# Side steps of the first new pair in two lines, and block 3's operands staged in four tiles

## The chip, the cores and the metric

The kernel runs on one core of a Trainium2 chip. The metric is the device time of one execution in microseconds (us), a median over runs. The engines are TensorE (PE; PEld is its weight load), VectorE (DVE), ScalarE (ACT), GpSimd (POOL), and SyncE (SP), whose queue issues almost all DMAs here.

## What is computed

Three layers in a row, all in fp32 (the reference, cut):

```
qn, kn = q / norm over tokens, k / norm over tokens         # q, k, v: 6016 x 256
a = softmax(kn.T @ qn / tau);  x = v @ a                    # a: 256 x 256
h = relu(x @ w_in);            x = (h * h) @ w_out          # 256 -> 2048 -> 256
xn = x / rms(x) * rms_g
out = (silu(xn @ w_gate) * (xn @ w_val)) @ w_out2           # 256 -> 1536 -> 256
```

## The kernel before

Tokens are columns. They are cut into 12 blocks (ten of 512 tokens, two of 448), and two blocks make a pair (pairs 0 to 5). `v @ a @ w_in` is folded: the softmax gives a weight `m_h`, `m_l` at the start, so that the first MLP is one product with `m`, relu, square, and one with `w_out`. Every fp32 product is made of three matmuls on split operands (a high part `h` from a cast on ScalarE and a rest `l` from a subtraction on VectorE): high x high, high x low, low x high.

The order of every engine's instructions is that of the code: nothing is rescheduled, and each engine works off its own list in order. The stages:

- Attention statistics and weight preparation, then blocks 0 and 1 of the first MLP, and blocks 2 to 7 one by one (`mlp1`, 16 units each: six matmuls of the first product, then six of the second product of the unit three back). Beside the units run side steps given by tables (`hooks`, `beside`: unit number to functions): the RMS norm of the block before (`norm_steps`), the preparation of the next block's operands from v (`prep`), weight conversion (`conv_steps`), and `pair_steps`: the seven combinations of a normed pair that the second MLP's Strassen-like product needs. Each combination is split into a tile (`hi`: cast on ScalarE, then a DMA to DRAM, `xd`; `lo`: subtraction on VectorE, then a second DMA). The tile comes from `staged(...)`, which goes round a list of places; `ys` names two buffers, `p0`, `p1`, `p6` one each. A cast into a buffer must wait until both DMAs out of its previous content are done.
- Blocks 8 and 9 (pair 4, the first "new pair", `FIRST`) and 10 and 11 (pair 5) go through `mlp1_pair`: eight groups of seven products and eight second products (`down`). A group has three places, `aside()`, where side steps are taken from the list `side`: after the second product, after the fifth, and at the end. In pair 4 the side steps are the norm of block 7, the `pair_steps` of pair 3, and `v_steps`, which make pair 5's seven operand combinations from v and send them to DRAM (`vd`) by tiles of the same `first_stage` list (`ys`, `p6`, `ys`, ...). `fill` mixed both kinds into one list, in turn; in pair 4 two steps were taken at some places.
- The second MLP, pairs 0 to 5 (`mlp2`, 12 groups each), with side steps in pair 0: the norm and combinations of pair 5 (`pair_side`) and the conversion of the last rows of `w_out2` (`rows_steps`: `a` on GpSimd and ScalarE, `b0` to `b2` on VectorE, `h`, `l`). In the group in which the norm's small matmul takes a PSUM bank (`takes_bank`, then `root`), `rooted` stopped all further side steps.

PSUM has four banks `mm`: bank 0 is each group's first product, the other three turn by one from group to group, so the copy into `bu` (L1492 in `mlp2`) goes to the bank that the group before read last as `bv` (L1526).

Of the kernel before, what the change touches and what calls it, by code (L numbers as in the profile page):

```python
# [28 lines left out]
def attn_moe_kernel(ctx: ExitStack, tc, q, k, v, tau, w_in, w_out, w_gate, w_val, w2, rms_g, out):  # L29
# [9 lines left out]
    _, N, C = q.shape  # L39
# [6 lines left out]
    q, k, v = q[0], k[0], v[0]  # L46
# [9 lines left out]
    FIRST = NP - 2  # L56
# [989 lines left out]
    def pair_steps(p, stage, fine=False):  # L1046

        n = blocks[2 * p][1]
        st = {}

        def sub(o, a, b):
            def f():
                x = [xst[p][:, i, :n] for i in (o, a, b)]
                nc.vector.tensor_tensor(out=x[0], in0=x[1], in1=x[2], op=ALU.subtract)

            return f

        def hi(i):
            def f():
                st[i] = stage()[:, :, :n]  # L1060
                nc.scalar.copy(out=st[i][:, 0], in_=xst[p][:, i, :n])  # L1061
                if p not in x_dram:
                    x_dram[p] = dp.tile([P, NC7, 2, NB], F32, tag=f"x{p}", name="xd")
                nc.sync.dma_start(out=x_dram[p][:, i, 0, :n], in_=f32(st[i])[:, 0])

            return f

        def lo(i):
            def f():
                t = st.pop(i)  # L1070
                nc.vector.tensor_tensor(out=t[:, 1], in0=xst[p][:, i, :n], in1=f32(t)[:, 0], op=ALU.subtract)  # L1071
                nc.sync.dma_start(out=x_dram[p][:, i, 1, :n], in_=f32(t)[:, 1])

            return f

        def both(*fs):
            return lambda: [f() for f in fs] and None

        if fine:
            return [  # L1080
                only("act", hi(0)), only("dve", sub(3, 2, 0)), both(lo(0), hi(4)), only("dve", sub(1, 6, 3)),
                both(lo(4), hi(6)), only("dve", sub(2, 6, 2)), both(lo(6), hi(3)), only("dve", sub(5, 4, 1)),
                both(lo(3), hi(1)), both(lo(1), hi(2)), both(lo(2), hi(5)), only("dve", lo(5)),
            ]
        return [
            both(hi(0), sub(3, 2, 0)), both(lo(0), hi(4), sub(1, 6, 3)), both(lo(4), hi(6), sub(2, 6, 2)),
            both(lo(6), hi(3), sub(5, 4, 1)), both(lo(3), hi(1)), both(lo(1), hi(2)), both(lo(2), hi(5)),
            lo(5),
        ]
# [102 lines left out]
    def v_steps(p, into):  # L1192


        b, n = 2 * p, blocks[2 * p][1]
        st, raw = {}, {}

        def loads(t):
            def f():
                raw[t] = load_v(b + t)  # L1200

            return f

        def tr(t, kk):
            def f():
                if t == 0 and kk == 0:
                    x = vp.tile([P, KC, NB], F32, tag="vt", name="vt")[:, :, :n]
                    st["x"] = {0: x[:, 0], 4: x[:, 1], 5: x[:, 0]}
                if t == 1 and kk == 0:
                    a, c = (place(k, F32)[:, :, :n] for k in (0, 1))  # L1210
                    st["x"].update({2: a[:, 0], 6: a[:, 1], 3: c[:, 0], 1: c[:, 1]})
                x = st["x"][SLOT[t][kk]]
                nc.vector.transpose(out=x.rearrange("p (g t) -> p g t", t=32), in_=raw[t][:, :, kk, :])

            return f

        def sub(o, x, y):
            def f():
                nc.vector.tensor_tensor(out=st["x"][o], in0=st["x"][x], in1=st["x"][y], op=ALU.subtract)

            return f

        def hi(i):
            def f():
                st[i] = into(i, n)
                nc.scalar.copy(out=st[i][0], in_=st["x"][i])

            return f

        def lo(i):  # L1230
            def f():
                h, l, store = st.pop(i)
                nc.vector.tensor_tensor(out=l, in0=st["x"][i], in1=f32(h), op=ALU.subtract)
                if store:
                    store()

            return f

        def seq(*fs):
            return lambda: [f() for f in fs] and None  # L1240

        return [
            loads(0), tr(0, 0), seq(tr(0, 1), loads(1)), hi(0), seq(lo(0), hi(4)), lo(4),
            seq(tr(1, 0), sub(3, 2, 0)), seq(tr(1, 1), sub(1, 6, 3)), seq(hi(3), sub(2, 6, 2)),
            seq(lo(3), hi(1), sub(5, 4, 1)), seq(lo(1), hi(2)), seq(lo(2), hi(6)), seq(lo(6), hi(5)), lo(5),
        ]

    def first_place(ops):
# [42 lines left out]
    def mlp1_pair(p, ops, side, after_product, after_group):  # L1291
# [43 lines left out]
        def group(g):  # L1335
# [5 lines left out]
                after_product(g, i)  # L1341

            def aside(k=1):
                for _ in range(k):
                    if side and not getattr(side[0], "takes_bank", False):
                        x = side.pop(0)()
                        if x:
                            x()

# [12 lines left out]
                old[2]()  # L1362
            down_slot()
            product(3, S1, bh, True)
            aside(2 if p == FIRST and g < G // 2 else 1)
            down_slot()
            product(1, S2, bu, False)
            uw = work(F32)[:, :, :n]
# [33 lines left out]
                r, q = x[:, 0], x[:, 1]  # L1402
            sums(TENSOR_ADD_SAT, out=r, in0=bh, in1=u, s0=FMAX, s1=0.0)
            lo()
            aside(2 if p == FIRST or g % 2 else 1)
            down_slot()
            left.append(square(r, q, f0, 1, False, last, 4))
            after_group(g)
# [7 lines left out]
    def mlp2(p, ops, after_product, after_group, side):  # L1416
# [17 lines left out]
        def group(f):  # L1434
# [26 lines left out]
            rooted = []  # L1461

            def aside(*only):
                if not side or rooted or getattr(side[0], "takes_bank", False):
                    return None
                e = getattr(side[0], "only", "")
                if not only or e in only:
                    side.pop(0)()
                    return e
# [205 lines left out]
    for b in range(2, 2 * FIRST):  # L1675
# [15 lines left out]
            else:  # L1691
                hooks = merge(hooks, {7: n0, 8: n1[:1], 9: n1[1:2], 10: n1[2:3], 13: n1[3:4], 14: n1[4:5], 15: n1[5:]})
        if b > 2 and b % 2:
            x = pair_steps(b // 2 - 1, staged("ys") if b == 3 else staged("ys", "p0", "ys", "p1"))
            beside = merge(beside, at_steps(x, {3: 4, 2 * FIRST - 1: 0}.get(b, 1)))
        if b < 2 * FIRST - 1:
            x = prep(b + 1)
            hooks = merge(hooks, {0: [load(b + 1)]} if b > 2 else {})
            at = (8, 9, 10, 11) if b % 2 else (3, 4, 8, 9)
            beside = merge(beside, {u: [f] for u, f in zip(at, x)})  # L1700
        else:
            beside.setdefault(0, []).append(third)
            x = v_steps(FIRST, first_place(ops1))
            for u in (0, 1, 3, 5, 6, 7, 8, 9, 10, 11, 12, 13, 14, 15):
                beside.setdefault(u, []).append(x.pop(0))
        for u in range(UNITS):
            if b in CONV:
# [11 lines left out]

    ops0 = {}  # L1720
    n0, n1 = norm_steps(2 * FIRST - 1, ys[2 * FIRST - 1])
    side = []

    def alternate(x, y):
        return [f for i in range(max(len(x), len(y))) for f in x[i : i + 1] + y[i : i + 1]]

    def fill():
        n = n0 + n1
        rest = side[:]
        k = len(n)  # L1730
        side[:] = alternate(n, rest[:k]) + pair_steps(FIRST - 1, first_stage) + rest[k:]

    drained.append(fill)
    first_stage = staged(*["ys", "p6", "ys"] * 4, "ys", "ys")
    for p in range(FIRST, NP):
        nxt = {}
        last = p == NP - 1
        if not last:
            side += v_steps(p + 1, through_dram(p + 1, first_stage))

        def after_product(g, i):
            if g == NF1 // 2 - 1:
                if not last and i in ORDER[3:]:
                    fetch_v(p + 1, i, nxt)
                if last and i == 0:
                    fetch(0, 4, ops0)

        def after_group(g):
            if g == 0 and p > FIRST:
                side.extend(pair_norm(p - 1) + pair_steps(p - 1, staged("ys", "p0", "ys", "p1")))  # L1750
            if not last and g == NF1 // 2 - 2:
                assert len(side) <= 4, len(side)
                for i in ORDER[:3]:
                    fetch_v(p + 1, i, nxt)
            if last:
                if g == 0:
                    nc.sync.dma_start(out=f32(gv_chunk(1)), in_=gv_dram[1])
                if g == NF1 // 2 - 2:
                    assert not side, len(side)
                    for i in ORDER[:3]:  # L1760
                        fetch(0, i, ops0)
                if g == NF1 // 2 - 1:
                    for i in (2, 5, 6):
                        fetch(0, i, ops0)

        mlp1_pair(p, ops1, side, after_product, after_group)
        ops1 = nxt
# [23 lines left out]
        ]  # L1791
    pair_side = pair_norm(NP - 1) + pair_steps(NP - 1, staged("vt", "ys", "vraw", "ys"), True)
    side = []
    side += pair_side[:6] + alternate(rows_steps, pair_side[6:])

    def load_w2(f, k):
        for j, x in enumerate("hl"):
# [5 lines left out]
    for p in range(NP):  # L1803
# [6 lines left out]
        def after_group(f):  # L1810
            if p == 0:
                if f == 0:
                    for x in "hl":
                        tiles[f"w2_{x}"] = wp.tile([P, NF2, KC, 4, 32], F32R, tag=f"w2_{x}", name=f"w2_{x}")
                    load_w2(0, 2 * EARLY)
                    late_calls[0].load()
                    for i in (2, 3, 4, 5):
                        nc.sync.dma_start(out=f32(gv_chunk(i)), in_=gv_dram[i])
            if f == 10 and p == 0:
# [61 lines left out]
```

## Time and profile before

| | us |
|---|---|
| median of 3 runs (lowest, highest) | 1134.37 (1133.78, 1135.11) |
| the profiled execution's own time | 1134.62 |
| span of its instructions | 1132.8 |
| PE busy / PEld busy | 1113.6 / 933.7 |
| DVE busy / ACT busy / POOL busy | 779.0 / 788.3 / 73.1 |

Busy time is what an engine spends in instructions; a matmul of the trace overlaps the next one (a row with 0.39 us stands 0.23 us before the next), so the start of a row tells more of the pace than its length. A row in brackets, `[3.67 <-DMA xd<-xp]`, says that the engine stood idle so long before the instruction and what ended it. Times are from the span's start.

### The profile page before, as it was taken

How to read it: one execution, taken by the hardware profiler on the slowest of the kernel's cores; microseconds unless marked ns; L12 is line 12 of the kernel's file. 1: busy time of each engine (PE TensorE's matmuls, PEld its weight loads, DVE VectorE, ACT ScalarE, POOL GpSimd, SP SyncE). 2: the span in 40 equal slices, each digit the busy share in tenths (PEclk: the TensorE clock that was granted, in tenths of full speed). 3: DMA queues.
4: the chain of work that ended last, by engine and by line, in shares of the span. 5: the costliest groups of instructions: out<-in, count | busy, mean ns of one | idle time of the engine just before them, and what ended most of it. 6: DMA issues, size and time to landing. Idle time of an engine off the chain costs nothing.

```text
span 1132.8 us, 14576 instructions
## 1 busy us (share of the span) xinstructions
PE 1113.6 (98%) x5170; PEld 933.7 (82%) x5170; DVE 779.0 (69%) x1194; ACT 788.3 (70%) x1428; POOL 73.1 (6%) x106
## 2 busy tenths in 40 slices
PE   8999999999999999999999999999999999999997
PEld 7978888877888888768997888888888888888996
DVE  6998768878878787766866875555555655655655
ACT  7688778778888787667778766556556566556554
POOL 2421102102111000000000000000000000000000
PEclk9999999999999999989999999999999999999999
DMA  9643321353343331135168242202302302202001
GB/s 327 221 112 95 111 71 60 112 180 99 132 148 102 122 100 49 63 143 185 45 207 343 62 150 79 84 1 75 93 1 75 93 1 75 68 19 66 19 19 34
DMA packets 103305, 114.47 MB, mean 101 GB/s; under 512 B 50368, under 2 KB 71872, under 8 KB 102592
## 3 DMA queue, kind: packets, MB, share of 16 engines
q1 hardware_dynamic: 100960, 112.68, 29.9%
q10 hardware_dynamic: 2272, 0.85, 0.3%
q8 instruction: 41, 0.67, 0.3%
q14 instruction: 32, 0.26, 0.1%
HBM read 71.83 MB, written 41.68 MB: 100 GB/s over the span
## 4 chain that ended last, share of the span: by engine, by line
PE 55%; DVE 1%; ACT 0%; DMA 0%; issue 0%; DVEq 0%; ACTq 0%
PE mm L1441 30%; PE acc L110 7%; PE acc L111 7%; PE acc L112 7%; PE mm L1339 4%; DMA vd<-xp 0%; PE acc L1569 0%; DVE xp L1071 0%; DMA xd<-xp 0%; DVE p L1326 0%; DVE sh L1329 0%; ACT xp L1061 0%; DVE p L1071 0%; ACT mm L1370 0%; DVE p L1382 0%
## 5 line engine op out<-in xcount | busy, mean ns | idle before, releaser
L1441 PE MATMUL mm<-p,gv 128*128 128x512 f32 (+1 forms) x1188 | 302.3, 387 | 0.0
L1441 PEld LDWEIGHTS mm<-p,gv 128*128 128x128 f32 x1188 | 221.7, 188 | 45.7 <-DVE hp L1517 1.1
L1542 DVE TENSOR_TENSOR sh<-hp,sh 128x512 fp32r<-128x512 f32 (+1 forms) x144 | 98.0, 681 | 138.2 <-ACT sh L1538 137.9
L1492 ACT COPY mm<-mm 128x512 f32<-128x512 f32 (+1 forms) x72 | 40.4, 562 | 172.2 <-PE mm L1441 163.0
L111 PE MATMUL acc<-sh,wo_h 128*128 128x512 f32 (+1 forms) x384 | 149.6, 390 | 2.9 <-DVE sh L849 2.2
L110 PE MATMUL acc<-sh,wo_h 128*128 128x512 f32 (+1 forms) x384 | 149.9, 390 | 1.1 <-ACT sh L1320 1.1
L112 PE MATMUL acc<-sh,wo_l 128*128 128x512 f32 (+1 forms) x384 | 148.9, 388 | 0.1
L849 DVE TENSOR_TENSOR sh<-p,sh 128x512 fp32r<-128x512 f32 x128 | 92.7, 726 | 55.3 <-ACT sh L842 48.9
L110 PE MATMUL acc<-sh,w_h 128*128 128x512 f32 (+1 forms) x284 | 109.5, 386 | 0.0
L112 PE MATMUL acc<-sh,w_l 128*128 128x512 f32 (+1 forms) x284 | 109.5, 385 | 0.0
L111 PE MATMUL acc<-sh,w_h 128*128 128x512 f32 (+1 forms) x284 | 109.5, 385 | 0.0
L837 ACT ACTIVATE p<-mm 128x512 f32<-128x512 f32 x128 | 76.0, 594 | 25.2 <-PE mm L112 24.9
L1538 ACT CAST sh<-hp 128x512 fp32r<-128x512 f32 (+1 forms) x144 | 89.1, 618 | 3.4 <-DVE hp L1526 1.9
L112 PE MATMUL mm<-p,m_l 128*128 128x512 f32 x224 | 87.5, 391 | 0.3 <-DVE m_l L773 0.3
L111 PEld LDWEIGHTS acc<-sh,wo_h 128*128 128x128 f32 x384 | 72.6, 189 | 18.5 <-DVE sh L849 4.4
L110 PE MATMUL mm<-p,m_h 128*128 128x512 f32 x224 | 87.3, 390 | 0.0
L111 PE MATMUL mm<-p,m_h 128*128 128x512 f32 x224 | 87.2, 389 | 0.0
L110 PEld LDWEIGHTS acc<-sh,wo_h 128*128 128x128 f32 x384 | 72.6, 189 | 15.0 <-ACT sh L1320 1.5
L112 PEld LDWEIGHTS acc<-sh,wo_l 128*128 128x128 f32 x384 | 72.5, 189 | 14.3 <-DVE wo_l L182 0.9
L1441 PE MATMUL mm<-xs,gv 128*128 128x512 f32 (+1 forms) x324 | 82.6, 381 | 0.0
L1526 DVE TENSOR_TENSOR hp<-mm,sg 128x512 f32<-128x512 f32 (+1 forms) x72 | 48.9, 679 | 44.3 <-PE mm L1441 44.3
L1517 DVE TENSOR_TENSOR hp<-mm,pu 128x512 f32<-128x512 f32 (+1 forms) x72 | 49.0, 681 | 30.0 <-ACT pu L1516 30.0
(249 smaller groups left out, 2080.3 us busy)
## 6 DMA issues: line engine op xcount, KB each, us to landing
p<-xd SPq DMA_DIRECT2D x58, 256.0 KB, 4.0
xd<-xp SPq DMA_DIRECT2D x46, 256.0 KB, 2.0
gv<-gvd SPq DMA_DIRECT2D x5, 1792.0 KB, 16.3
gvd<-gp SPq DMA_DIRECT2D x15, 512.0 KB, 3.3
xd<-p SPq DMA_DIRECT2D x24, 256.0 KB, 2.2
raw<-in_moe_w_out_dram SPq DMA_DIRECT2D x11, 512.0 KB, 3.7
out_dram<-ot SPq DMA_DIRECT2D x40, 128.0 KB, 2.3
qraw<-in_q_dram SPq DMA_DIRECT2D x13, 384.0 KB, 7.2
```

The source lines that it names most:

```text
L110: nc.tensor.matmul(o, wh, xh, start=start, stop=False)
L111: nc.tensor.matmul(o, wh, xl, start=False, stop=False)
L112: nc.tensor.matmul(o, wl, xh, start=False, stop=stop)
L837: nc.scalar.activation(out=r, in_=o, func=AF.Relu)
L849: nc.vector.tensor_tensor(out=sl, in0=s, in1=f32(sh), op=ALU.subtract)
L1339: nc.tensor.matmul(bank, m_part(a, w, g), x, start=start and j == 0, stop=j == 2, skip_group_check=not start)
L1441: nc.tensor.matmul(bank, c[:, hl, a, fs], x, start=start and j == 0, stop=j == 2, skip_group_check=not start)
L1492: cp(out=bu, in_=b0)
L1517: add(out=h22, in0=bh, in1=w, op=ALU.add)
L1526: dve(out=h21, in0=bv, in1=sg1, op=ALU.mult)
L1538: nc.scalar.copy(out=parts[t][0], in_=x)
L1542: dve(out=pl, in0=x, in1=f32(ph), op=ALU.subtract)
```

## The change

- Pair 4's side steps stand in two lists, `side` (norm and `pair_steps`) and `tokens` (`v_steps`); a place takes one of each, but only one step that casts into a staging tile (`staged`): the second waits for the next place. In pair 5 the same rule holds for the two steps of a place.
- `v_steps` has 15 steps (its `lo(1)` and `hi(2)` are apart); block 7, which runs the same steps by a table, takes two of them at unit 11.
- Block 3's `pair_steps` go round `ys, p0, ys, p1` (four buffers) in place of `ys` alone (two). `p0` and `p1` hold block 4's operands later, so their splits in `prep` move from units 10 and 11 to 12 and 13.
- In pair 0 of `mlp2`, VectorE-only steps may follow the root in the same group; the first late row is converted earlier, and its load stands ahead of `load_w2`.

```
@@ mlp1_pair
             def aside(k=1):
-                for _ in range(k):
-                    if side and not getattr(side[0], "takes_bank", False):
-                        x = side.pop(0)()
+                staged = False
+                for q in [side] * k + [tokens]:
+                    if q and not getattr(q[0], "takes_bank", False):
+                        if staged and getattr(q[0], "staged", False):
+                            break
+                        f = q.pop(0)
+                        staged = getattr(f, "staged", False)
+                        x = f()
                         if x:
                             x()
...
             product(3, S1, bh, True)
-            aside(2 if p == FIRST and g < G // 2 else 1)
+            aside()
...
             lo()
-            aside(2 if p == FIRST or g % 2 else 1)
+            aside(1 + (p > FIRST and g % 2))
@@ v_steps
-            seq(lo(3), hi(1), sub(5, 4, 1)), seq(lo(1), hi(2)), seq(lo(2), hi(6)), seq(lo(6), hi(5)), lo(5),
+            seq(lo(3), hi(1), sub(5, 4, 1)), lo(1), hi(2), seq(lo(2), hi(6)), seq(lo(6), hi(5)), lo(5),
@@ mlp2
             def aside(*only):
-                if not side or rooted or getattr(side[0], "takes_bank", False):
+                if not side or getattr(side[0], "takes_bank", False):
                     return None
                 e = getattr(side[0], "only", "")
+                if rooted and e != "dve":
+                    return None
@@ blocks 2 to 7
         if b > 2 and b % 2:
-            x = pair_steps(b // 2 - 1, staged("ys") if b == 3 else staged("ys", "p0", "ys", "p1"))
+            x = pair_steps(b // 2 - 1, staged("ys", "p0", "ys", "p1"))
...
-            at = (8, 9, 10, 11) if b % 2 else (3, 4, 8, 9)
+            at = (8, 9, 12, 13) if b == 3 else (8, 9, 10, 11) if b % 2 else (3, 4, 8, 9)
...
-            for u in (0, 1, 3, 5, 6, 7, 8, 9, 10, 11, 12, 13, 14, 15):
+            for u in (0, 1, 3, 5, 6, 7, 8, 9, 10, 11, 11, 12, 13, 14, 15):
@@ pairs 4 and 5
-    def fill():
-        n = n0 + n1
-        rest = side[:]
-        k = len(n)
-        side[:] = alternate(n, rest[:k]) + pair_steps(FIRST - 1, first_stage) + rest[k:]
-
-    drained.append(fill)
+    side, tokens = [], []
+    drained.append(lambda: side.extend(n0 + n1 + pair_steps(FIRST - 1, first_stage)))
...
-            side += v_steps(p + 1, through_dram(p + 1, first_stage))
+            tokens += v_steps(p + 1, through_dram(p + 1, first_stage))
@@ side steps of pair 0 in mlp2
-    side += pair_side[:6] + alternate(rows_steps, pair_side[6:])
+    x, y = rows_steps[1:], pair_side[6:]
+    side += pair_side[:5] + rows_steps[:1] + pair_side[5:6] + [f for i in range(max(len(x), len(y))) for f in x[i : i + 1] + y[i : i + 1]]
...
+                    late_calls[0].load()
                     load_w2(0, 2 * EARLY)
-                    late_calls[0].load()
```

TensorE's list is the same in both kernels. Three places where the other lists differ (line numbers of the changed kernel are a few higher).

**ScalarE in block 3, units 9 to 11.** L837 begins a unit's evacuation, L1061 is the cast of `hi`, L106 the cast of block 4's operand. Before:

```order
L1061 CAST xp<-xst 128x512
L837 ACTIVATE p_828<-mm 128x512
L841 ACTIVATE p_829<-p_828 128x512
L842 CAST sh<-p_829 128x512
L1061 CAST xp<-xst 128x512
L106 CAST p_2328<-vt 128x512
L837 ACTIVATE p_828<-mm 128x512
L841 ACTIVATE p_829<-p_828 128x512
L842 CAST sh<-p_829 128x512
L106 CAST p_2329<-vt 128x512
L145 ACTIVATE raw<-raw 128x512
```

and now:

```order
L1061 CAST p_2301<-xst 128x512
L837 ACTIVATE p_828<-mm 128x512
L841 ACTIVATE p_829<-p_828 128x512
L842 CAST sh<-p_829 128x512
L1061 CAST xp<-xst 128x512
L837 ACTIVATE p_828<-mm 128x512
L841 ACTIVATE p_829<-p_828 128x512
L842 CAST sh<-p_829 128x512
L145 ACTIVATE raw<-raw 128x512
L837 ACTIVATE p_828<-mm 128x512
L845 ACTIVATE sh<-p_828 128x512
L106 CAST p_2373<-vt 128x512
```

Every second cast of `hi` goes to a tile `p`, and the two casts L106 stand two units later.

**ScalarE in pair 4, the end of one group and the start of the next.** L1393 (now L1410) reads the sixth product, L1358 (now L1375) is the next group's first copy, L1226 a cast of `v_steps`, L1061 one of `pair_steps`. Before, from the end of group 3 on:

```order
L1393 ACTIVATE p_4014<-mm 128x512
L1320 ACTIVATE sh<-p_4014 128x512
L1324 ACTIVATE p_4015<-p_4014 128x512
L1226 CAST xp<-p_4252 128x448
L1061 CAST p_4362<-xst 128x512
L1358 COPY mm<-mm 128x512
L1320 ACTIVATE sh<-p_4014 128x512
L1061 CAST xp<-xst 128x512
L1370 COPY mm<-mm 128x512
L1371 COPY sh<-mm 128x512
```

and now the same stretch:

```order
L1410 ACTIVATE p_4014<-mm 128x512
L1332 ACTIVATE sh<-p_4014 128x512
L1336 ACTIVATE p_4015<-p_4014 128x512
L1061 CAST xp<-xst 128x512
L1375 COPY mm<-mm 128x512
L1332 ACTIVATE sh<-p_4014 128x512
L1061 CAST xp<-xst 128x512
L1387 COPY mm<-mm 128x512
L1388 COPY sh<-mm 128x512
```

Each place now casts into one staging tile where this one cast into two.

**VectorE in pair 4, group 2, and in pair 0 of `mlp2`, group 2.** L929 is the reciprocal of the norm, L1213 (now L1219) a transpose of v, L1329 (now L1341) the rest `l` of the square that the next group's first `down` reads. Before:

```order
L1382 ISA p_4013<-mm,sh 128x512
L929 RECIPROCAL ns<-ns 128x16
L1213 STREAM_TRANSPOSE p_4251<-vraw 128x448
L1219 TENSOR_TENSOR p_4252<-p_4251,vt 128x448
L1329 TENSOR_TENSOR sh<-p_4015,sh 128x512
```

and now, with the norm's transpose L938 between:

```order
L1399 ISA p_4013<-mm,sh 128x512
L929 RECIPROCAL ns<-ns 128x16
L938 STREAM_TRANSPOSE p_4095<-p_4095 128x512
L1219 STREAM_TRANSPOSE p_4214<-vraw 128x448
L1225 TENSOR_TENSOR p_4215<-p_4214,p_4215 128x448
L1341 TENSOR_TENSOR sh<-p_4015,sh 128x512
```

In `mlp2`, L998 is the reciprocal of the root and L1526 (now L1545) the product that reads the bank `bv`. Now:

```order
L1536 TENSOR_TENSOR hp<-mm,pu 128x512
L998 RECIPROCAL ns<-ns 128x28
L149 TENSOR_SCALAR sg<-sg 128x512
L153 ISA sg<-pu,sg 128x1024
L1545 TENSOR_TENSOR hp<-mm,sg 128x512
```

L149 and L153 (the late row's first conversion) stood two groups further on.

## Rows read from the trace of the kernel before

**Rows 1.** The page, part 1: busy time of each engine (share of the span).

```profile
PE 1113.6 (98%) x5170; PEld 933.7 (82%) x5170; DVE 779.0 (69%) x1194; ACT 788.3 (70%) x1428; POOL 73.1 (6%) x106
```

**Rows 2.** Waits of TensorE over the span: us in total, times, longest.

```profile
PE mm L1339 <- ACT mm L1358: 2.2, 1, 2.2
PE acc L111 <- DVE sh L849: 2.2, 4, 1.1
```

**Rows 3.** Busy time in three stretches of pair 4: stretch, length, engines, PEclk, DMA.

```profile
455.50:465.70 10.20, 10.20 (x46) 8.45 (x45) 9.46 (x16) 7.51 (x15) 0.00 (x0) 1.00 0.00 0
475.90:480.00 4.10, 2.27 (x8) 1.28 (x8) 1.29 (x2) 3.29 (x7) 0.00 (x0) 0.98 0.22 84
480.00:490.60 10.60, 8.38 (x21) 5.99 (x20) 4.40 (x7) 4.29 (x9) 0.00 (x0) 0.53 0.38 148
```

**Rows 4.** TensorE in order of time: first matmuls of groups 5, 6, 7 and of pair 5.

```profile
475.96 0.39 PE L1339 MATMUL mm<-vx,m_h 128*128 128x512 f32 x1
...
494.76 0.39 PE L1339 MATMUL mm<-vx,m_h 128*128 128x512 f32 x1
...
505.90 0.39 PE L1339 MATMUL mm<-vx,m_h 128*128 128x512 f32 x1
...
516.10 0.36 PE L1339 MATMUL mm<-p,m_h 128*128 128x448 f32 x1
```

**Rows 5.** SP and ScalarE in order of time, pair 4, group 5.

```profile
474.62 0.32 SPq L1072 DMA_DIRECT2D xd<-xp  x1
...
476.68 0.62 ACT L1061 CAST xp<-xst 128x512 fp32r<-128x512 f32 x1 [3.67 <-DMA xd<-xp]
```

**Rows 6.** Busy time in block 3's late units and block 4's first.

```profile
240.00:261.00 21.00, 18.84 (x78) 13.90 (x77) 17.41 (x25) 17.91 (x32) 4.93 (x6) 1.00 0.45 140
```

**Rows 7.** Waits of ScalarE from 218 to 262 us.

```profile
ACT xp L1061 <- DMA xd<-xp: 6.7, 4, 2.7
```

**Rows 8.** TensorE in order of time: the same matmul of a unit, six units apart.

```profile
240.66 0.39 PE L110 MATMUL mm<-p,m_h 128*128 128x512 f32 x1
...
261.07 0.39 PE L110 MATMUL mm<-p,m_h 128*128 128x512 f32 x1
```

**Rows 9.** Pair 0 of mlp2 in order of time: ScalarE, VectorE and TensorE.

```profile
606.94 0.57 ACT L1492 COPY mm<-mm 128x512 f32<-128x512 f32 x1 [1.81 <-DVE hp L1526]
...
615.28 0.58 ACT L1492 COPY mm<-mm 128x512 f32<-128x512 f32 x1
...
614.14 0.63 DVE L1526 TENSOR_TENSOR hp<-mm,sg 128x512 f32<-128x512 f32 x1
...
621.71 0.42 DVE L149 TENSOR_SCALAR sg<-sg 128x512 int32<-128x512 int32 x1
622.25 0.69 DVE L153 CUSTOM_DVE_ANT_0 sg<-pu,sg 128x1024 uint16<-128x1024 uint16 x1
...
616.09 1.55 PE L1441 MATMUL mm<-p,gv 128*128 128x512 f32 x6
```

**Rows 10.** The late row's load: SP, landing of all three, and TensorE's first matmul with w_l.

```profile
593.27 0.48 SPq L134 DMA_DIRECT2D pu<-in_moe_w_out_dram  x1
...
DMA to landing us min/median/max: 3.5/4.1/9.0
...
603.59 0.39 PE L112 MATMUL acc<-sh,w_l 128*128 128x512 f32 x1
```

**Rows 11.** VectorE and TensorE in order of time: block 7's norm, and pair 4's group 2.

```profile
420.89 0.24 DVE L929 RECIPROCAL ns<-ns 128x16 f32<-128x16 f32 x1
...
422.46 0.65 DVE L844 TENSOR_TENSOR p<-p 128x512 f32<-128x512 f32 x1
...
453.99 0.68 DVE L1329 TENSOR_TENSOR sh<-p,sh 128x512 fp32r<-128x512 f32 x1
...
456.42 0.39 PE L111 MATMUL acc<-sh,wo_h 128*128 128x512 f32 x1
```

More of the change, by code (lines that the diff above doesn't have):

```diff
@@ L1064, in f @@
                 nc.sync.dma_start(out=x_dram[p][:, i, 0, :n], in_=f32(st[i])[:, 0])
+            f.staged = True
             return f
@@ L1076, in both, with g @@
         def both(*fs):
-            return lambda: [f() for f in fs] and None
+            def g():
+                for f in fs:
+                    f()
+            g.staged = any(getattr(f, "staged", False) for f in fs)
+            return g
         if fine:
@@ L1226, in f @@
                 nc.scalar.copy(out=st[i][0], in_=st["x"][i])
+            f.staged = True
             return f
@@ L1239, in seq, with g @@
         def seq(*fs):
-            return lambda: [f() for f in fs] and None
+            def g():
+                for f in fs:
+                    f()
+            g.staged = any(getattr(f, "staged", False) for f in fs)
+            return g
         return [
@@ L1721, in attn_moe_kernel @@
     n0, n1 = norm_steps(2 * FIRST - 1, ys[2 * FIRST - 1])
-    side = []
-    def alternate(x, y):
-        return [f for i in range(max(len(x), len(y))) for f in x[i : i + 1] + y[i : i + 1]]
-    def fill():
-        n = n0 + n1
-        rest = side[:]
-        k = len(n)
-        side[:] = alternate(n, rest[:k]) + pair_steps(FIRST - 1, first_stage) + rest[k:]
-    drained.append(fill)
+    side, tokens = [], []
+    drained.append(lambda: side.extend(n0 + n1 + pair_steps(FIRST - 1, first_stage)))
     first_stage = staged(*["ys", "p6", "ys"] * 4, "ys", "ys")
@@ L1751, in after_group @@
             if not last and g == NF1 // 2 - 2:
-                assert len(side) <= 4, len(side)
+                assert not side and len(tokens) <= 3, (len(side), len(tokens))
                 for i in ORDER[:3]:
```

## The prediction

> **What bounds the kernel now.** The page comes first: TensorE is busy 1113.6 of 1132.8 us, the next engine 788.3 [rows 1]. So the end moves only by what TensorE stands still or runs slowly, and a step on another engine costs nothing as long as TensorE does not wait for it. Next I asked where it waits. Apart from the start (the first 80 us, which the change does not touch) the list of waits holds two places: pair 4 in `mlp1_pair`, where a matmul waited 2.2 us for ScalarE's copy L1358, and the end of block 3, where four second products waited 2.2 us in sum for VectorE's L849 [rows 2].
>
> Pair 4: the stretches show group 3 running at 10.20 us with TensorE never idle; then 1.83 us of 4.10 are idle in one stretch and 2.22 of 10.60 in the next, and there the granted clock is 0.53, that is mostly the lower level of 1.2 GHz; elsewhere it is 1.00 [rows 3]. The reader is to see both in the starts of the groups: group 7 takes 505.90 to 516.10 = 10.20 us, which is the pace, but groups 5 and 6 together take 475.96 to 505.90 = 29.94 us, **9.54 us too long** [rows 4].
>
> What holds ScalarE there? A cast into a `ys` tile. VectorE's `lo` of the tile's previous content is done and its store is issued at 474.62; the cast starts when it has landed, at 476.68, after 3.67 us of standing still [rows 5]. Behind that cast in ScalarE's list are the square that the next second product reads, then the copy that the next product needs: TensorE waits, VectorE waits for ScalarE, the next `lo` and its store come later, and the next cast later still.
>
> Block 3 has the same cause earlier: four casts waited 6.7 us for stores [rows 7], because `ys` alone gives a tile back after two units. ScalarE falls behind, and when the conversion of weights fills it and VectorE some units later (17.91 and 17.41 of 21 us) TensorE runs dry [rows 6]. Its idle time there is 21.00 - 18.84 = 2.16 us [rows 6]. But I size the loss from starts: the same matmul of a unit stands at 240.66 and, six units later, at 261.07, that is 20.41 us [rows 8]. A unit is 12 matmuls, and a group has 45 in 10.20 us [rows 4], so six units take 16.32: **4.09 us too long**.
>
> The Trainium skill (Perfetto Trace Analysis, Identifying the Most-Contended Engine) says that matmul busy share is a poor measure of headroom and weight-load busy share a good one. It holds here: weight loads are 8.45 of 10.20 us at full pace and 13.90 of 21.00 in this stretch [rows 3, 6], which would make 4.2 us lost, near the 4.09; by idle time alone the sum below would be 1123.7 in place of 1121.8.
>
> **The change, part by part.** TensorE's list stays as it is, so every gain is a wait taken away.
>
> 1. *One staging tile at a place, two lists.* The three tiles of `first_stage` go round, and a group has three places, so a tile is asked for again one group later, about 10 us. Cast, `lo` at the next place (about 3.4 us on), store (474.62 to 476.68, 2.06 us [rows 5]): some 6 us, 4 to spare. The tightest is a `ys` tile whose `lo` stands at the middle place and which the next group's first place wants: seven of a group's fifteen slots of 0.68 us lie between, 4.8 us, and ScalarE has a copy and a square before it (1.1 us), against two steps of VectorE ahead of the store (1.2 us), 0.5 us of issue and the store's 2.1 us or a little more: 1 to 2 us to spare. I take all of it: -9.54, waits, the low clock and the restarts. Bounds: -9.54 if no cast waits; about -3.5 if a shorter wait returns and the clock falls again (rival 1).
>
> 2. *VectorE is fuller in groups 2 and 3.* It was busy 9.46 of 10.20 us in group 3 [rows 3] already. In group 2 the norm's transpose now stands ahead of the v transpose and of `lo` L1329. The pair reciprocal and transpose with ScalarE's copy between took 420.89 to 422.46 = 1.57 us [rows 11]. So `lo`, at 453.99, starts at most at 455.56 and ends at 456.24. The matmul that reads it starts at 456.42 [rows 11], its weight load some 0.2 us before: it just fits, or is late by a little. In group 3, seven side steps of VectorE (16 instructions in 9.46 us [rows 3] make 0.59 each) put the same `lo` as close. Bounds: 0 to 0.3 us at each of the two; I take +0.2 in sum.
>
> 3. *Block 3 in four tiles.* A tile comes back after four units (10.9 us) in place of two (5.4), so the 6.7 us of waits go. The two splits of block 4 move to units 12 and 13, into the fuller stretch, and add two casts (0.5 us each) and two subtractions (0.6 each) there, where ScalarE would now be early by most of 6.7 us. They must end before block 4's first matmul, three units on. Of the 4.09 us some 0.15 stay, the norm's two small matmuls. I take -3.94. Bounds: -2 (half of the lateness is VectorE's conversion, not the tiles) to -4.09.
>
> 4. *Pair 0 of `mlp2`.* L149 and L153 now stand behind the reciprocal and ahead of L1526 in the root's group. Their busy times are 0.42 + 0.69 us [rows 9], so L1526 moves from 614.14 to 615.25 and ends at 615.94. The next group's copy into `bu` waits for it (in the group before it waited 1.81 us for just this [rows 9]): it starts at 615.94, not 615.28, and with 0.57 us ends at 616.51. TensorE wants that bank at 616.09 [rows 9]: +0.45 (0.42 and a restart). Bounds: 0, if the end of the copy counts less than its busy time, to 0.7. What is queued behind the copy on ScalarE shifts by as much and hides in its idle time. The late row's load, now first: before, it was issued at 593.27 as the last of the three and took 9.0 us, so all three are in by 602.3 in either order, and the first matmul that wants `w_l` is at 603.59 [rows 10]: nothing, unless the queue gives up 1.3 us.
>
> 5. *Block 7 (two steps at unit 11) and pair 5 (deferred casts)*: TensorE does not wait there before, and VectorE gets 0.6 us one unit earlier: nothing, covered by the three-unit lag of the second products.
>
> Sum, against the profiled execution's 1134.62 us: -9.54 + 0.2 - 3.94 + 0.45 = -12.83, so 1121.8. The median of the runs is 0.25 lower, so **1121.5**.
>
> **Rivals.**
>
> 1. *New short waits bring the low clock back once.* For it: in pair 4 the clock fell right after TensorE had stood 1.83 us in one short stretch [rows 3], and part 2 leaves next to no margin at two group ends. Against it: in block 3 it stood 2.16 us in 21 and kept 1.00 [rows 6]. Price: of the 9.54 us, 1.83 + 2.22 = 4.05 were idle in the two stretches [rows 3]; the other 5.5 are the clock, the restarts and a last short wait. I take 5.0 for the clock and restarts, and 1.0 of new waits: 1127.5. The Trainium skill (TensorE: Matmul & The Clock Gate, A second HAM failure mode: psum-queue depth-cycling) describes this: frequent micro-idles between groups make the clock swing. By that rule waits as short as part 2's could be enough; block 3's stretch speaks against it.
>
> 2. *Block 3 stays late.* The conversion on VectorE, not the tiles, holds it, and the moved splits add to it. For it: VectorE is busy 17.41 of 21 us [rows 6]. Price: 2 us of the gain: 1123.5.
>
> 3. *One of the two places does not do what it says*: the casts wait for something else than their tile. Against it: the waits name the stores [rows 5, 7]. Price: pair 4 alone missing, 1131; block 3 alone missing, 1125.5. Both missing is no change.
>
> 4. *Slower.* One mechanism: the short waits of part 2 come at each of pair 4's eight group ends, since VectorE never catches up. A spell at the low clock costs the same 5.0 + 1.0 us; slower than before needs more than 12.8 us above the forecast, so from the third spell on, 1140 or so. Against it: outside groups 2 and 3 the lists have at most five side steps in a group, with the group's own eight or nine 14 instructions of 0.59 us, 8.3 of 10.2 us, so VectorE catches up in group 4.
>
> **How the numbers follow.** No change here means within 0.2% (2.3 us), about what a measurement of this kernel can tell. The forecast (1120.6 to 1123.2): 0.67. Rival 1: 0.13. Rival 2: 0.09. Rival 3: 0.05 with one place missing, 0.03 with both (no change). Rival 4: 0.03. Faster is all but the last two, 0.94. The forecast and rival 2 hold 0.76, so the range reaches to rival 1: 1120.4 to 1127.8, which leaves out some 0.11. The low end is every cost at nothing, the rest of the small matmuls included.
>
> **What would show it.** In the changed profile: the granted clock at 1.00 through pair 4 and its groups at 10.2 us each; no cast L1061 or L1226 waiting for a store there or in block 3; block 3's six units near 16.4 us; no wait of TensorE for L849; one wait of some 0.4 us for ScalarE's copy in `mlp2`, pair 0, group 3; perhaps one or two below 0.3 us for a `lo` at the start of pair 4's groups 3 and 4. I am wrong if a stretch at 0.5 shows up in pair 4, if a cast still waits over 1 us for a store, or if VectorE's transposes of pair 4 push a second product by more than 0.5 us.

## The result, and the profile after

The changed kernel takes 1121.96 us (median of 4 runs, 1120.95 to 1122.38) against 1134.08 (4 runs, 1133.78 to 1135.11): ratio 0.989, 95% interval 0.9873 to 0.9907. The forecast was 1121.5, in a range of 1120.4 to 1127.8. The profiled execution took 1122.16 us, its span is 1120.5.

The page, part 1 (answers to [rows 1]), and all waits of TensorE that the profile names after the first 85 us (answers to [rows 2]; us in total, times, longest):

```profile
PE 1107.9 (99%) x5170; PEld 931.7 (83%) x5170; DVE 779.8 (70%) x1194; ACT 789.6 (70%) x1428; POOL 74.5 (7%) x106
```

```profile
PE mm L1458 <- ACT mm L1511: 0.3, 1, 0.3
```

Both waits of before are gone, and one that was not there has come, in `mlp2`.

**Pair 4.** The stretches of groups 3, 4, 5 and 6 (as [rows 3]) and the first matmuls of groups 5, 6, 7 and of pair 5 (as [rows 4]):

```profile
451.49:461.69 10.20, 10.20 (x47) 8.45 (x45) 9.86 (x17) 8.17 (x16) 0.00 (x0) 1.00 0.19 72
461.69:471.89 10.20, 10.20 (x47) 8.45 (x45) 9.73 (x16) 8.25 (x16) 0.00 (x0) 1.00 0.50 191
471.89:482.09 10.20, 10.20 (x47) 8.45 (x45) 7.76 (x13) 8.33 (x16) 0.00 (x0) 1.00 0.39 151
482.09:492.29 10.20, 10.20 (x47) 8.45 (x45) 6.93 (x12) 7.79 (x15) 0.00 (x0) 1.00 0.32 125
```

```profile
471.89 0.39 PE L1351 MATMUL mm<-vx,m_h 128*128 128x512 f32 x1
...
482.09 0.39 PE L1351 MATMUL mm<-vx,m_h 128*128 128x512 f32 x1
...
492.29 0.39 PE L1351 MATMUL mm<-vx,m_h 128*128 128x512 f32 x1
...
502.49 0.36 PE L1351 MATMUL mm<-p,m_h 128*128 128x448 f32 x1
```

Groups 3 to 7 take 10.20 us each, with no idle time and the clock at 1.00: groups 5 and 6 take 20.40 us where they took 29.94. And no cast waits for a store any more (where [rows 5] had 3.67 us); these are all waits of ScalarE from 415 to 505 us, and the ones for TensorE mean that ScalarE is early:

```profile
ACT mm L1387 <- PE mm L1351: 9.6, 7, 2.1
ACT p L1391 <- PE mm L1351: 3.0, 8, 1.0
ACT mm L1375 <- PE mm L1351: 2.8, 4, 0.9
ACT sh L1332 <- DVE p L1399: 2.8, 6, 0.8
ACT p L937 <- DVE ns L929: 1.6, 2, 0.8
```

**Block 3.** The same matmuls as in [rows 8], six units apart, and ScalarE's waits from 216 to 262 us (as [rows 7]):

```profile
240.49 0.39 PE L110 MATMUL mm<-p,m_h 128*128 128x512 f32 x1
...
257.06 0.39 PE L110 MATMUL mm<-p,m_h 128*128 128x512 f32 x1
```

```profile
ACT gp L211 <- DVE dg L157: 2.7, 1, 2.7
ACT p L837 <- PE mm L112: 2.0, 6, 0.5
ACT p L937 <- DVE ns L929: 0.8, 1, 0.8
```

16.57 us in place of 20.41, and no line `<- DMA` is left. L837 now waits for TensorE: the order of who waits for whom has turned.

**`mlp2`, pair 0, group 2 and the start of group 3** (as [rows 9]): VectorE, ScalarE, TensorE in order of time.

```profile
601.37 0.36 DVE L149 TENSOR_SCALAR sg<-sg 128x512 int32<-128x512 int32 x1
601.77 0.69 DVE L153 CUSTOM_DVE_ANT_0 sg<-pu,sg 128x1024 uint16<-128x1024 uint16 x1
602.38 0.68 DVE L1545 TENSOR_TENSOR hp<-mm,sg 128x512 f32<-128x512 f32 x1
```

```profile
603.15 0.57 ACT L1511 COPY mm<-mm 128x512 f32<-128x512 f32 x1 [0.54 <-DVE hp L1545]
```

```profile
603.09 0.39 PE L112 MATMUL acc<-sh,w_l 128*128 128x512 f32 x1
603.77 1.65 PE L1458 MATMUL mm<-p,gv 128*128 128x512 f32 x6 [0.30 <-ACT mm L1511]
```

The late row's two instructions (before, one group further on, at 621.71 [rows 9]) push L1545 (L1526 before); the copy waits 0.54 us for it, and TensorE's next product starts 0.68 us after the matmul ahead of it in place of 0.23: 0.45 us.

### The profile page after: what moved, and what is told of

Same layout as the page of the kernel before. It is cut to its first block, busy times and chain, and to the rows that moved or that the text cites. A ratio compares the mean times of both kernels' runs of the same rounds, so it can differ in the third digit from the quotient of the medians.

```text
span 1120.5 us, 14578 instructions
## 1 busy us (share of the span) xinstructions
PE 1107.9 (99%) x5170; PEld 931.7 (83%) x5170; DVE 779.8 (70%) x1194; ACT 789.6 (70%) x1428; POOL 74.5 (7%) x106
## 4 chain that ended last, share of the span: by engine, by line
PE 90%; ACT 3%; DVE 2%; DMA 2%; POOL 1%; issue 1%; SPq 0%; DVEq 0%; ACTq 0%
PE mm L1458 29%; PE acc L110 13%; PE acc L112 13%; PE acc L111 13%; PE mm L1351 6%; PE mm L111 5%; PE mm L112 5%; PE mm L110 5%; POOL rows L569 1%; DMA qraw<-in_k_dram 1%; DMA rraw<-in_v_dram 1%; PE mm L761 1%; ACT ws L592 0%; ACT hl L609 0%; DVE dg L153 0%
## 5 line engine op out<-in xcount | busy, mean ns | idle before, releaser
L849 DVE TENSOR_TENSOR sh<-p,sh 128x512 fp32r<-128x512 f32 x128 | 92.8, 727 | 53.5 <-ACT sh L842 47.3
L837 ACT ACTIVATE p<-mm 128x512 f32<-128x512 f32 x128 | 76.1, 594 | 27.6 <-PE mm L112 27.1
L1545 DVE TENSOR_TENSOR hp<-mm,sg 128x512 f32<-128x512 f32 (+1 forms) x72 | 49.0, 680 | 43.3 <-PE mm L1458 42.9
```

Source lines behind the costliest of these rows:

```text
L837: nc.scalar.activation(out=r, in_=o, func=AF.Relu)
L849: nc.vector.tensor_tensor(out=sl, in0=s, in1=f32(sh), op=ALU.subtract)
L1545: dve(out=h21, in0=bv, in1=sg1, op=ALU.mult)
```

## The experiments

Eleven kernels ran, each beside the kernel before on the same chip; differences are those of medians on that chip. Where few runs stand beside many, the ratio can say about 1 us more or less than the medians; there the starts in the trace decide.

**1. Block 3 alone.**

```
-staged("ys") if b == 3 else staged("ys", "p0", "ys", "p1")
+staged("ys", "p0", "ys", "p1")
-at = (8, 9, 10, 11) if b % 2 else (3, 4, 8, 9)
+at = (8, 9, 12, 13) if b == 3 else (8, 9, 10, 11) if b % 2 else (3, 4, 8, 9)
```

> The kernel before with block 3's edit alone: four staging tiles, and block 4's two splits moved to units 12 and 13. The forecast (the tiles come back late, and nothing else holds block 3): 3.8 to 3.9 us less than before, so 1130.2 where before is 1134.1; no cast L1061 waits for a store there, no second product waits for VectorE's L849, six units take about 16.5 us. Rival 2 (the conversion on VectorE holds it): only 2 us less, 1132.1, with waits for L849 left. Pair 4 must lose its 9.5 us as before.

Measured: 1130.57 against 1134.42, ratio 0.9966 (0.9956 to 0.9976): -3.85 us. No wait for L849, none of L1061 for a store; the six units take 16.56 us. The term of the sum holds alone: the trace's 16.56 us are the forecast's "about 16.5", and the median is within 0.1 us of it, in an interval of 2.7 to 5.0 us.

**2. Pairs 4 and 5 alone**: the two lists, the rule, `v_steps` with 15 steps and block 7's unit 11; the rest as before.

> The kernel before with the edits of pairs 4 and 5 alone (two lists, one staging tile at a place, lo(1) and hi(2) apart, block 7's two steps at unit 11). The forecast: 9.3 to 9.5 us less, 1124.7 where before is 1134.1, granted clock 1.00 in all of pair 4, its groups 10.2 us each; block 3's four waits for L849 (2.2 us) are still there. Rival 1 (short waits bring the low clock back): 1129 to 1130. If the gains of the two places add up, this saving and that of block 3 alone make 13.2 to 13.4 us.

Measured: 1124.95 against 1134.42, ratio 0.9906 (0.9887 to 0.9925): -9.47 us. L849's four waits are still there (2.2 us). The ratio alone would make 10.7 us of it; by the starts, pair 4 takes 81.92 us where the kernel before takes 91.52, 9.60 less. The two savings alone make 13.32 by medians.

**3. The splits alone**: the second line pair of run 1 without the first.

> The kernel before with only block 4's two splits moved to units 12 and 13; the staging tiles of block 3 stay two. If the tiles' return sets the pace (the forecast), the four casts still wait some 6 to 7 us for stores, and the time changes by at most 1 us either way (the casts that moved had stood among the waiting ones). If the crowd of work at units 10 and 11 was the cause (rival 2), most of the 3.9 us goes: 1130 to 1131.

Measured: 1134.12 against 1134.42, ratio 0.9996 (0.9986 to 1.0006). The casts wait as long as before (first fence: ScalarE, 218 to 262 us), and the moved split is now late for block 4's first product (second fence: TensorE):

```profile
ACT xp L1061 <- DMA xd<-xp: 6.8, 4, 2.9
```

```profile
247.17 0.49 PE L110 MATMUL mm<-p,m_h 128*128 128x512 f32 x1 [0.87 <-ACT p L106]
...
259.31 0.50 PE L111 MATMUL acc<-sh,wo_h 128*128 128x512 f32 x1 [1.14 <-DVE sh L849]
```

So moving the crowd of work away from units 10 and 11 gives nothing by itself: the tiles are needed. What the four tiles would give without the moved splits no run shows, since `p0` and `p1` are the places of those splits. Rival 2 (VectorE's conversion holds block 3) is out by run 1, which left the conversion as it was and got the whole term back.

**4. A fourth tile in pair 4 in place of the two lists.**

```
-first_stage = staged(*["ys", "p6", "ys"] * 4, "ys", "ys")
+first_stage = staged("ys", "p6", "ys", "ys", "p6", "ys", "p2", "ys", "p6", "ys", "p2", "ys", "ys", "p2")
```

> The kernel before, its one mixed list with two steps at a place left as it is, but from pair 4's seventh cast on a fourth staging tile stands in the ring of first_stage. If the late return of a tile is what stalled pair 4 (the forecast's reading), the casts that waited 3.7 and 3.4 us for stores in groups 5 and 6 start at once, the clock stays at 1.00, and 7.5 to 9.5 us go: 1124.6 to 1126.6 where before is 1134.1. If it is the two steps at a place that load ScalarE and VectorE, the loss stays: 1132 to 1134.

Measured: 1128.15 against 1134.42, ratio 0.9937 (0.9920 to 0.9954): -6.27 us, 1.2 less than the low end; by the starts pair 4 takes 84.63 us in place of 91.52, 6.89 less. The casts into the tiles `p` start at once. But a place with two casts (477.13 and 477.64) still uses up the ring, the cast at 481.94 waits 2.64 us for a store, and TensorE waits twice (its rows, and the stretch of group 5):

```profile
483.10 0.96 PE L1339 MATMUL mm<-vr,c 128*128 128x512 f32 x3 [1.19 <-ACT mm L1370]
494.33 0.98 PE L1339 MATMUL mm<-vr,c 128*128 128x512 f32 x3 [0.62 <-ACT mm L1370]
```

```profile
476.10:487.90 11.80, 10.61 (x47) 8.28 (x46) 8.75 (x15) 8.60 (x17) 0.00 (x0) 1.00 0.46 178
```

Two things follow. The tile's return is the cause of most of the loss, since the order of the steps is that of before; what is left (2.7 us) goes, by the trace, with the two casts at one place, but no run takes that away by itself. And the clock stayed at 1.00 with a wait of 1.19 us by itself.

**5. The changed kernel without the rule.** The two lines with `break` go.

```
-                        if staged and getattr(q[0], "staged", False):
-                            break
```

> The changed kernel without the rule of one staging tile at a place: the two lists stay, so a place may cast into two tiles, and a tile of the three is wanted again one place later, 3.4 us, against the 6 us that cast, rest and store take. The forecast's reading: casts wait 2 us and more for stores in pair 4's groups 4 and 5, TensorE waits some 2 to 4 us, and if the clock falls as before 5 us more: 1124 to 1131 where the changed kernel is 1122. Rival: the two lists were what helped, and the rule does nothing: within 0.5 us of the changed kernel.

Measured: 1129.44, where the changed kernel on the same chip (run 6) has 1124.04: 5.40 us slower; against the kernel before 0.9943 (0.9928 to 0.9957). ScalarE's casts, TensorE's waits, and the stretch behind them:

```profile
468.59 0.57 ACT L1232 CAST xp<-p 128x448 fp32r<-128x448 f32 x1 [1.98 <-DMA xd<-xp]
...
475.50 0.57 ACT L1232 CAST p<-vt 128x448 fp32r<-128x448 f32 x1 [3.18 <-DMA xd<-p]
```

```profile
469.70 0.97 PE L1351 MATMUL mm<-vr,c 128*128 128x512 f32 x3 [2.30 <-ACT mm L1385]
...
476.64 0.49 PE L110 MATMUL acc<-sh,wo_h 128*128 128x512 f32 x1 [1.11 <-ACT sh L1332]
477.89 0.50 PE L111 MATMUL acc<-sh,wo_h 128*128 128x512 f32 x1 [0.76 <-DVE sh L1341]
```

```profile
479.00:484.00 5.00, 5.00 (x17) 3.89 (x16) 3.54 (x6) 3.13 (x7) 0.00 (x0) 0.69 0.61 235
```

Without the rule the two lists lose more than half of pair 4's gain again (by the starts pair 4 takes 88.90 us in place of 81.97). It is the same chain as before, store, cast, square, matmul, beginning one group earlier. It is the rule that spaces the casts.

**6 to 8. The changed kernel again, and `mlp2`'s part taken back.** Run 7 has `rooted`, the order of `side` and the place of the load as before. Run 8 keeps the change but for one line ahead of `product(5, ...)`:

```
-            if f:
+            if f and not rooted:
                 asides()
```

> The changed kernel itself, beside which the next two are read. 12.1 us less than before, as it was.

> The changed kernel with mlp2's part of the change taken back (no step behind the root, the late row's load and conversion where they stood). The forecast's fourth term: the one wait of 0.3 us for ScalarE's copy in pair 0, group 3, goes, and the time is 0.45 to 0.55 us below the changed kernel. The rival, that the earlier conversion gives the 0.45 back later in pair 0: no difference within 0.1 us.

> The changed kernel, but in the root's group of mlp2 the two instructions of the late row may stand only behind the product that reads the bank bv, no longer ahead of it. If the wait comes from that one place (the forecast), it goes as in the run before, 0.45 to 0.55 us below the changed kernel. If two more instructions of VectorE anywhere in that group are too many, a wait of 0.2 us or more shows for the sum or the silu that stand behind them.

Measured on one chip, where before takes 1135.72: the changed kernel 1124.04 (1123.21 to 1124.64; ratio 0.9893, 0.9877 to 0.9910), run 7 1122.30 (1122.05 to 1123.13; 0.9880, 0.9866 to 0.9895), run 8 1122.60 (1122.33 to 1122.96; 0.9882, 0.9867 to 0.9897). Run 7 is 1.74 us below the changed kernel, and no single time of the one reaches the other; the two ratios' intervals overlap. The wait for the copy is gone in both. The 0.45 to 0.55 are too little, and the traces say what else there is. SP issues the loads of pair 1's first operands, in run 6, then in run 7:

```profile
664.53 1.43 SPq L1134 DMA_DIRECT2D xs<-xd  x3
```

```profile
658.19 1.40 SPq L1134 DMA_DIRECT2D xs<-xd  x3
```

and TensorE's first products of pair 1, in the same order:

```profile
669.53 0.85 PE L1458 MATMUL mm<-xs,gv 128*128 128x512 f32 x3
670.61 0.96 PE L1458 MATMUL mm<-xs,gv 128*128 128x512 f32 x3 [0.23 <-DMA xs<-xd]
```

```profile
668.89 1.52 PE L1458 MATMUL mm<-xs,gv 128*128 128x512 f32 x6
```

With the changed list the last combinations of pair 5 are cast and stored some 6 us later, the loads stand behind these stores in SP's queue, and a product that should follow after 0.68 us follows after 1.08. From the first copy of pair 0 to that of pair 2, run 6 takes 181.93 us, run 7 180.87, run 8 181.14: of the 1.74 us the trace places 1.06 here, some 0.5 for each of the two waits. The two profiled executions, 1124.15 and 1123.13, are 1.02 apart, so that is all of their difference; the further 0.7 of the medians no trace shows, and it is within the scatter of single runs (1.1 to 1.4 us). Run 8 is 1.44 us below the changed kernel by medians, of which its trace places 0.79: the copy's wait is gone, the loads come late as in run 6 (issued at 663.32).

**9. `mlp2`'s part alone**, on the kernel before.

> The kernel before with mlp2's part of the change alone (VectorE-only steps may follow the root, the first late row earlier, its load first). By the forecast's fourth term it is 0.45 to 0.55 us slower than before, all of it at the copy into bu in pair 0, group 3. By what the traces of the changed kernel and of the one with mlp2 as before show, there is a second cost: the side steps of pair 0 end one group later, so the loads of pair 1's first operands are issued some 6 us later and its first product waits 0.2 to 0.6 us: 0.8 to 1.1 us slower in all. If that second cost came only with the other edits, no wait for a load shows here.

Measured: 1134.99 against 1134.52, ratio 1.0006 (0.9997 to 1.0015): +0.47, too small for a verdict of its own: the interval takes in both expectations, and no change too. The trace has the wait of 0.29 us for the copy, and xs<-xd issued at 676.81 in place of 671.08. No wait for a load is named, but pair 1's first three product steps are 0.7 us longer in sum. So the late loads come with this part and not with the others; that they make those steps longer is read from the place and not from a named wait.

**10 and 11. Waits made on purpose**, of two sizes, in the changed kernel (5 stands in the first, 9 in the second): the repeats write the same values again.

```
+            for _ in range(5 if p == FIRST and g == 5 else 1):
                 cp(out=bu, in_=b0)
```

> The changed kernel with four idle repeats of ScalarE's first copy L1375 at the start of pair 4's group 5 (0.48 us each, 1.9 us in sum; the copy has 1.3 us to spare ahead of the product that reads it). TensorE should wait some 0.6 us at one place. If only long standing brings the clock down, the granted clock stays at 1.00 and the time is 0.6 us above the changed kernel, about 1122.6. Rival 1 in its strong form (a short wait is enough): the clock falls to 0.5 for some 10 us, and the time is 5 to 6 us above it, about 1127.5.

> The same with eight repeats (3.8 us): TensorE should wait 2.5 us at one place, more than the two waits after which the clock fell in the kernel before. If the sum of standing time decides, the clock falls to 0.5 and the time is 2.5 + 5 = 7.5 us above the changed kernel, about 1129.5; if not, 2.5 above, about 1124.5. And if the pace of pair 5's last groups (9.12 us in kernels whose clock fell in pair 4, 9.30 in those where it did not) hangs on the spell, it is 9.12 here when the clock falls.

Measured: 1123.92 (ratio to before 0.9899, 0.9870 to 0.9928) and 1128.89 (0.9946, 0.9923 to 0.9968), 11.6 and 6.6 us below before, where the changed kernel is 11.7 to 12.1 below. TensorE's wait in the first, then in the second kernel with what comes behind it, and two stretches of the second:

```profile
475.61 0.50 PE L1351 MATMUL mm<-vx,ch 128*128 128x512 f32 x1 [1.03 <-ACT mm L1376]
```

```profile
478.23 0.50 PE L1351 MATMUL mm<-vx,ch 128*128 128x512 f32 x1 [3.43 <-ACT mm L1376]
...
480.52 0.63 PE L1351 MATMUL mm<-vr,m_h 128*128 128x512 f32 x1
480.94 0.63 PE L110 MATMUL acc<-sh,wo_h 128*128 128x512 f32 x1
```

```profile
479.60:483.00 3.40, 3.40 (x10) 2.67 (x9) 1.53 (x3) 1.93 (x4) 0.00 (x0) 0.53 0.40 154
483.00:490.00 7.00, 7.00 (x32) 5.71 (x31) 5.78 (x10) 5.52 (x10) 0.00 (x0) 0.99 0.24 91
```

One wait of 1.03 us leaves the clock alone: group 5 takes 11.53 us, 1.33 more than its pace. After one of 3.43 it falls to 1.2 GHz, but for 3.4 us only; the matmuls stand 0.42 us apart there in place of 0.23. Group 5 takes 15.57 us: 3.7 of the extra 5.37 are the wait and its restart, the other 1.7 the clock, where the expectation had 5 for it. Both waits came out longer than expected (0.6 and 2.5), because a repeat took 0.60 us and not 0.48: nine copies take 5.38 us, five 2.98.

## Why the prediction was right, point by point

**What bounds the kernel.** Right: every us of the gain is a wait of TensorE or a spell at the low clock that went, and the two places of [rows 2] hold all of it. The start of the same matmul in both traces shows where it comes from: -0.20 us ahead of block 3, -3.82 in it, nothing from there to pair 4, -9.59 in pair 4, +0.83 in pair 5, +0.60 in `mlp2` up to its third pair, nothing further: -12.2, where the forecast had -12.83.

**Term 1, pair 4 (-9.54).** Right, in mechanism and size: -9.59 in the trace, -9.47 timed alone. Runs 4 and 5 show the cause from both sides: if a tile is wanted again later (a fourth tile) most of the loss goes without the lists, and if it is wanted earlier (no rule) more than half of it is back with them.

What the sum did not get right is the share of the low clock. Runs 3 and 9 leave pair 4 as it was. In their executions the clock stayed at 1.00 until TensorE had waited longer for the copy, and was low for 3.4 us only, where the kernel before had some 10 [rows 3]; run 3, then run 9:

```profile
484.78 0.50 PE L1339 MATMUL mm<-vx,ch 128*128 128x512 f32 x1 [3.33 <-ACT mm L1358]
```

```profile
475.90:485.40 9.50, 4.33 (x17) 2.70 (x16) 4.47 (x8) 5.47 (x10) 0.00 (x0) 1.00 0.36 140
485.50:488.90 3.40, 3.40 (x10) 2.64 (x9) 1.11 (x2) 0.19 (x1) 0.00 (x0) 0.50 0.28 107
```

```profile
483.89 0.66 PE L1339 MATMUL mm<-vx,ch 128*128 128x512 f32 x1 [3.34 <-ACT mm L1358]
```

Yet from group 5's first matmul to that of pair 5 they take 40.18 and 40.17 us, the kernel before 40.14, and the cast that waits 3.42 us for a store starts 12.53 to 12.56 us after that matmul in all three. So almost 7 us less of the low level gave nothing back: ScalarE's casts, held by the stores, set the pace, and what the clock did not take TensorE waited. In run 1's execution, with two spells of 3.4 us, the same stretch takes 41.17. The term came out right because it was sized from starts, whatever the shares.

**Term 2, VectorE in groups 2 and 3 (+0.2).** Its bound was right, the value taken too high: nothing is waited for. The `lo` that was to start at most at 455.56 of the old time axis starts at 451.38 + 4.02 = 455.40 on it, and the matmul that reads it starts 1.01 us behind that, 0.32 behind the `lo`'s end:

```profile
451.38 0.69 DVE L1341 TENSOR_TENSOR sh<-p,sh 128x512 fp32r<-128x512 f32 x1
```

```profile
452.39 0.39 PE L111 MATMUL acc<-sh,wo_h 128*128 128x512 f32 x1
```

**Term 3, block 3 (-3.94).** Right: -3.82 to -3.85. It was sized from starts and not from idle time; idle time alone (2.16 us [rows 6]) would have given little more than half. The Trainium skill (Perfetto Trace Analysis, Identifying the Most-Contended Engine) prefers weight loads' busy share to matmul's, and by that share 4.2 us were lost; the 3.84 found stand near it.

**Term 4, `mlp2` (+0.45).** The wait was forecast with its place, its cause and its size (measured 0.45 us at the next product, and 0.1 in its six matmuls). One addition in its sum is off: L1526, started at 615.25 with 0.63 us, ends at 615.88 and not 615.94, so the sum makes 0.39. The step that failed is the one beside it, that nothing else in `mlp2` costs: the list of side steps also has an end, and the loads of pair 1's operands stand behind its last stores. In all seven traces with that list these loads are issued some 6 us later, and pair 1 takes 0.2 to 0.8 us longer (runs 5, 6, 8, 9, 10 and 11, and the changed kernel's first trace). That the late row's load costs nothing where it stands is borne out: no wait names it.

**Term 5, block 7 and pair 5 (nothing).** Right for block 7: between block 4 and pair 4 the two traces keep their distance of 4.02 us. In pair 5 no wait appears either; the +0.83 there is no effect of the change (last section).

**Rivals.** Rival 1's trigger did not come, and its price was too high. 5.0 us for the clock were taken from a spell that had a further wait of 2.23 us in it and lay where the stores set the pace (term 1); with one wait and nothing behind it the fall cost 1.7 us (run 11; eight matmuls 0.2 us too far apart make 1.6 in run 5). By that price its time, with the 1.0 of waits that it took, would have been 1124.2 and not 1127.5. Waits of 1.03 and 1.19 us alone left the clock at 1.00, and a wait of 1.1 us with one of 0.75 right behind it brought it down in three traces of five (last section). The Trainium skill (TensorE: Matmul & The Clock Gate, A second HAM failure mode) has frequent micro-idles make the clock swing; the traces agree in so far as two short waits close together could do it. Rival 2 fell with run 1, and run 3 took away the crowd at units 10 and 11 as a cause. Rival 3 and rival 4 did not occur. Against rival 4 the forecast had VectorE catch up in group 4, at some 8.3 of 10.20 us; that was wrong: it was busy 9.86 us in group 3 and 9.73 in group 4, and caught up in group 5 (7.76). TensorE waited for none of it, with little to spare.

The median came 0.46 us above the forecast. By the one profiled execution that is the late loads (0.2) and the pace of pair 5 (0.8), less the 0.2 of term 2 that were not needed and 0.2 ahead of block 3, which the change does not touch.

## What to carry to other kernels

Where a cast into a staging tile waits for the store of its previous content, count the casts between two uses of a tile and the time from cast to landed store: either more tiles (6.9 of 9.6 us here) or fewer casts at a place (all of it) gives the time back, and a rule on the order costs no memory. Size a loss by the starts of the same instruction one period apart, and not by idle time, which misses the restarts and the low clock; and do not price the low clock apart where another engine sets the pace. When a list of side steps is reordered, follow it to its last step as well: what is queued behind that step (here the next pair's loads) moves with it. And the version to keep is run 7, the two lists and the four tiles without `mlp2`'s part: 1.06 us by the trace, 1.74 by medians.

## What the hardware showed that was not expected

**Which waits brought the clock down.** Single waits of 1.03 us (run 10), 1.19 (run 4) and 1.88 (run 1) left the granted clock at 1.00, and so did one of 2.30 (run 5) for the 5.8 us up to the next wait, and four that sum to 2.16 us in 21 [rows 6]. One of 3.43 (run 11) brought it down, and so did one of 2.06 in run 1, 3 us behind that of 1.88. A wait of 1.07 to 1.12 us with one of 0.74 to 0.76 behind it, one matmul between them, ended both ways: the clock fell in the kernel before and in runs 1 and 5, and stayed at 1.00 in runs 3 and 9, where it fell only with a further wait of 3.33 and 3.34. So the same waits do not end the same way in every execution, and these runs give no size of a wait that is safe. Each fall came within 1.6 us of TensorE's start after a wait. The low level lasted 3.4 us in runs 3, 5, 9 and 11 and in each of the two spells of run 1, and some 10 us in the kernel before, with another wait of 2.23 us in it [rows 3].

**Two paces of 448-column matmuls.** In the changed kernel's first profile the groups 4 to 6 of pair 5 take 9.30 us, in its second profile 9.12, with TensorE busy throughout, the granted clock at 1.00 and no wait; first profile, then second, the first matmuls of groups 6 and 7:

```profile
558.75 0.37 PE L1351 MATMUL mm<-p,m_h 128*128 128x448 f32 x1
...
568.05 0.37 PE L1351 MATMUL mm<-p,m_h 128*128 128x448 f32 x1
```

```profile
559.21 0.37 PE L1351 MATMUL mm<-p,m_h 128*128 128x448 f32 x1
...
568.33 0.37 PE L1351 MATMUL mm<-p,m_h 128*128 128x448 f32 x1
```

The matmuls stand 0.207 us apart in the one and 0.2025 in the other. In the last pair of `mlp2`, also 448 columns, it is the other way about: 6.69 us a group in the first profile, 6.82 in the second. Stretches with 512 columns have one pace, 0.227. It is 0.8 and 1.2 us of a run and belongs to the execution, not to the kernel. The guess that it hangs on a spell at the low clock in pair 4 does not hold: run 11 has 9.30 with a spell, and runs 6 to 8 have 9.12 without one. What sets it stays open.
